# Attention and two feed-forward layers on one core: the first chunks' queries and keys loaded as 512 columns per half of the rows instead of 640 with zeros, and a new order of the program

## The chip, the cores and the metric

One Trainium2 chip; the program runs on one of its NeuronCores. A core has a matrix engine (TensorE, PE in the profile), a vector engine (VectorE, DVE), a scalar engine (ScalarE, ACT), a general engine (GpSimd, POOL) and a queue engine (SyncE, SP), which here issues every DMA. Each engine runs its own instructions in order and waits for the others by semaphores. The metric is the device time of one execution in microseconds, lower is better. The kernel before takes 863.84 us, the median of three runs (863.59 to 864.96).

## The reference

Block-causal attention (blocks of 64 positions) over 4 batches, 8 heads, 576 positions and 64 columns per head; then two feed-forward layers over the 2304 tokens, 512 wide, 2048 in between.

```python
scores = scale * np.matmul(q, k.transpose(0, 1, 3, 2))
scores = np.where(block_i >= block_j, scores, -1000000000.0)
attn = softmax(scores)                    # max subtracted, sum + 1e-9
x = np.matmul(attn, v)                    # heads put side by side: 2304 x 512
h = x @ w_in
x = (h * np.tanh(softplus(h))) @ w_out    # first layer
return np.square(np.maximum(x @ w_in2, 0)) @ w_out2   # second layer
```

All inputs and the output are float32.

## The kernel before

*Work.* The tokens go in six chunks of 384 through two layers, in twelve passes (`PASSES`). The first two chunks hold, of each batch, the first 192 positions (`LO`), and the other four the last 384 of one batch (`HI`). Attention of a `LO` chunk is done by `attention_lo` in float32, one pair of heads at a time: 2 chunks x 2 batches x 4 pairs are 16 calls. `HI` chunks go through `attention_hi`, with 16-bit high and low parts. A layer's products are also formed of 16-bit high and low parts, three matmuls each (L1352, L1464; L1385 and L1503 in the passes with seven products in place of eight), except for the first pieces of the first pass, in float32 (L1416, L1430). Weights arrive as packed integers, are decoded on DVE and ACT (L1149, L1150), weighed, split and written back to DRAM.

*One pair of heads in `attention_lo`.* L1042 loads queries and keys, 128 rows (64 per head) of 640 columns, L1043 the values. The columns are three blocks of queries (128 each) and the keys (64 and 192). A block of queries holds one head's columns in its 64 rows and zeros, which come with the load, in the other 64, so that a matmul over all 128 rows gives one head's scores (L1054; the third block has 64 queries of either head). L1055 adds the mask. DVE takes the maxima (L1059, L1060) and makes them the bias (L1061), ACT does three exponentials (L1064), DVE the reciprocal sums (L1067, L1069), ACT or DVE the scaling (L823, L825). Four transposes (L1077 to L1080) go through PE, L791 or L793 copies them out, and L1092 and L1093 multiply by the values.

*Buffers.* The loads of L1042 have six buffers (`R["qkl"]`), two in the tensor `qk` and four in `vs`, so the seventh load waits for the first scores. `qk` and `vs` are later reused by `attention_hi`.

*Order.* No loop sets the order. Every instruction is a task with an engine and dependences; a table (`PLAN`) gives the order of all tasks and the engine of those that could run on several (`planned`, L386). The table is unpacked at build time, and each engine gets its instructions in that order. `FIRST`, `SLACK`, `URGE` and the costs in `sch.add` belong to the planner that ran without the table; they don't act on the built program.

Of the kernel before, what the change touches and what calls it, by code (L numbers as in the profile page):

```python
# [68 lines left out]
def seg_len(tiles):  # L69
# [34 lines left out]
    ";%|0Ul6|_5RWHeL^qr0^BRJ(Jxlgw1vwDHvFT>G%pZ3K^dvpV9Ht20Klr@`msN5{uSoJwNZPpv4uUxHz<r%q77V1@UtNg21qxTcoxKdZ?3cX&wl~=IwRe2q`"
    "FS4q>T*2!La<^QD|1Oo;dJ?|6T?WaAaw#$BB30yZX(dm{bX}ki<JpCp1D3|<IQfxJKj;8?LE6bZSldEo>O}ojTg!O;T|0w>CuFStq7CFrovc4<Q|T>l$!Ge#"
    "*2TK}rG`w@Q940C)P7i4Q$EnUh|feUxm||o=Q;*oca}HsSY!EEn<MKLb(Xy<BlI2_qP68c^dGKY>Ye!W9q{u98g)aHf%xSOWdDLTqqT$d!nfB+Wuy86$Uj@|"
    "CE~fJ2k5$-b%*u8#NZNg;W6T{Pan}2vHJ$e0Ac&Jqud9sddfh32qfLD2jl>|d&pxT_L!{KR&oh`Ze|LIOdlDb*MpyX^g3-|dP{p*C%g4VEx@MLa=G@=m2$Oo"
    "*DbnC_SxQgNV{oQyt+Yq>U_!Jc}z3S0O`O<?Q|CV`^gq<t8=w2R^2Wa>NFW99mt+p`28lb;dAtCCS#?o_LBd}Tyo}GITN3@)PL~ujnYF}Xm1%uwiIDu6a7S9"
    "<*&o~2`C#v9{<2&nvNoVAIf}PA#ck-d0!@J8&FqSXMr7&cccZ#pRVKd4R$w?Ux~nIusxLhZ^~<?sZ5lQ^m!T2l^4xI`<6b7?Du(n9{pzMP%!zKJPPI>1Dh}F"
    "2gG%Zenv)?<Fu#sBORv0<Vj9?TOTL#uY=r_JdEwX+M)WO%(JyY%WI%_fc#gU(`q24KX+f$XXGifRi8v|F<Ee>Tx|02=5W0XX=~8^0qR;$PJUd5lIsu2BhrQQ"  # L110
    "9+G}kz9sl$lRipTEx^0|xw8%ruhjv1HNO2<`-A6pWYm3n7r30Jcj!RybhqBh?v~)brQAt{nT>aQfzKKG08wg$$7hnm`@!Yq+DU%Wp2YtSa<RX*lMBhUV{)^O"
    ")SKmYG~1vT>cya^vtFTZ>$Ti(qrKSGNM1#^Q)PjkPHh~?s&mEVTq7#z#YD1`oG0gl>QkhhZpNQA&AG(?9O};5c(5&3+mf|y<#at0UC-7$GP;#C*GAO0#?pt1"
    "IEXtpp>+f5PdRy#E5&&6bYfe`)u!?vEhW`JXCpkgl*~H?+4pKc?)BHxB%4pCQqw=gXCuKt6}f^MogyF4BnPamiMH0ZK-)TS&R{;*qMjbLzfyT$lR{gSx?WGq"
    "NL^T=A_&+H4{X!&GTJ-=+8-iUGl|Lrl4r}~y(84-dt|M>mwP#~#@;PuL2F;UcQ**?2lw;^XXVM!JBY1Nb)J&~+Xss-MD|TcI);p6$n8ay7+@YDL$=_pRb+a9"
    "BJvKXDzHna(PQm);xU~po~HBk4%w;Q&}|11*+EslN!~Tvz)gF0PjH^L)j`YuV1oI&#7?2=EwY<*67^s`o}54g*XrMPjdrDGt|oV8+V*f$C;3a;Qv>TFr#YyZ"
    "58u?{Qx|zaenI1Eaxr<>Le8gV=Tn{9%XgeLi)c?k=QG){9u{mxmYgH4<qPy(NyY9Cc50B5lhJsxj-_T*qDB^=?YC6lue2e49H|{_H#wWUtcSNhqu!own^QZ_"
    "Al`X;AB;6Z*OII6>%aOEIu6r|=o%Uj`)qdAk!Oi<8FUj6w-sx9V&zb3r4s+=K*n1AT`CfRhIlpyPp<&CkAZ=c$+Wuc{EseVZF_Xv&igj7XvnX>i2GP@b4<UH"
    "Hppm56)r=@ucDeC&`rmC>w82wm-^61-jzD!rotn0i0BsBvk3m~j`W)Nye7UWP1YZz+H|I(??r<Pq_RAX?SrtP5KrWj?`5cxkD%!W?Aed4v$SbYoebHfGw4<f"
    "`53^a4S2oXYyKhLIS6OXhw<0Iyz_WpK;F**5!>*6iX9f)en+SIuuQ37D@>n>2YSG%ztBCbq#mtO$ELsO74%dWakY>~9yMSSJXc5s8Vhpr@a=jkZ)x=0Ps9uL"
# [1779 lines left out]
```

## Time and profile before

| | |
|---|---|
| median of 3 runs | 863.84 us (863.59 to 864.96) |
| profiled execution: time, span | 863.41 us, 861.6 us |
| PE, DVE, ACT, POOL busy | 845.8, 759.8, 614.9, 63.2 us |
| PE weight loads busy | 606.5 us |
| DMA moved, mean rate | 217.24 MB, 252 GB/s |
| span in 40 slices, PE busy tenths | 7, then 38 of 9, then 7 |

The profile is one execution. Busy time is the time in which an engine has an instruction in it. Matmuls are pipelined, so a busy PE is not a PE at its peak; yet where it is busy all the time, another engine's delay has not reached it. DMA-issuing instructions don't count as busy for SP. Where an engine waited, the profile names the engine or the transfer that came last. The line numbers are those of the kernel before.

### The profile page before, as it was taken

To read this page: it belongs to the slowest core of one execution; us is meant where nothing else is said; L and a number is where in the kernel's file an instruction comes from. 1 tells how busy PE (TensorE), PEld (TensorE's weight loads), DVE (VectorE), ACT (ScalarE), POOL (GpSimd) and SP (SyncE) were. 2 spreads that over 40 slices of the span, in tenths; PEclk is the share of its full clock that TensorE was granted. 3 is DMA by queue.
4 is the path that set the end of the run, shared out by engine and by line. 5 is a ranking of instruction groups with operands and counts; after the bars stand their busy time and mean duration, and the time that the engine had idled before them with its cause. 6 is when DMAs were issued, how large, how long until landed. Compare 5 with 4: busy or idle time off the path is not lost.

```text
span 861.6 us, 19020 instructions
## 1 busy us (share of the span) xinstructions
PE 845.8 (98%) x7233; PEld 606.5 (70%) x7233; DVE 759.8 (88%) x1836; ACT 614.9 (71%) x1224; POOL 63.2 (7%) x70
## 2 busy tenths in 40 slices
...
GB/s 340 382 330 221 208 247 223 279 312 284 260 286 221 258 231 226 246 247 285 272 302 273 306 260 263 269 253 227 209 220 291 225 190 212 258 244 252 186 214 73
DMA packets 163931, 217.24 MB, mean 252 GB/s; under 512 B 107520, under 2 KB 125952, under 8 KB 163840
## 3 DMA queue, kind: packets, MB, share of 16 engines
...
q8 instruction: 56, 0.92, 0.4%
...
## 4 chain that ended last, share of the span: by engine, by line
PE 73%; ACT 6%; DVE 5%; DMA 4%; issue 1%; SPq 0%; ACTq 0%; DVEq 0%
PE acc L1464 28%; PE hp L1385 23%; PE hp L1352 10%; PE acc L1503 5%; PE bank L1018 3%; PE bank L909 2%; PE bank L1503 2%; DMA wspill<-arena 1%; DMA arena<-wspill 1%; ACT pad L933 1%; DVE st L922 1%; DVE arena L818 1%; DMA pt<-pb 1%; ACT h L1357 1%; DVE pb L818 1%
## 5 line engine op out<-in xcount | busy, mean ns | idle before, releaser
L1464 PE MATMUL acc<-g,arena 128*128 128x384 f16 x1560 | 301.5, 326 | 0.7 <-DMA arena<-wspill 0.7
L1464 PEld LDWEIGHTS <-arena 128*128 128x128 f16 x1560 | 147.1, 98 | 83.8 <-issue 3.4
L1385 PEld LDWEIGHTS <-arena 128*128 128x128 f16 x1194 | 101.1, 98 | 15.2 <-issue 1.5
L1352 PE MATMUL hp<-xt,first 128*128 128x384 f16 x528 | 102.7, 326 | 1.9 <-ACT h L1357 1.8
L818 DVE SCALAR_TENSOR_TENSOR g<-h,cst,g 128x768 f16<-128x768 f32 x72 | 73.7, 1024 | 6.9 <-ACT g L1121 4.0
L1352 PEld LDWEIGHTS <-first 128*128 128x128 f16 x528 | 49.5, 98 | 42.0 <-issue 10.9
L1385 PEld LDWEIGHTS <-first 128*128 128x128 f16 x816 | 69.5, 98 | 7.4 <-issue 0.5
L818 DVE SCALAR_TENSOR_TENSOR pb<-pad,st,pb 128x384 f16<-128x384 f32 (+2 forms) x96 | 71.6, 754 | 2.8 <-ACT pb L953 2.5
L933 ACT ACTIVATE pad<-bank,st,sq 128x448 f32<-128x448 f32 (+1 forms) x96 | 65.0, 680 | 12.6 <-DVE sv L839 4.9
L1352 PE MATMUL hp<-xt,arena 128*128 128x384 f16 x384 | 73.8, 326 | 0.0
L1385 PE MATMUL hp<-arena 128*128 128x192 f16 x660 | 67.3, 246 | 0.0
L953 ACT ACTIVATE pb<-pad,st 128x384 f16<-128x384 f32 (+2 forms) x81 | 57.1, 716 | 5.5 <-DVE st L945 2.5
L1406 ACT ACTIVATE h<-h,cst 128x576 f32<-128x576 f32 x40 | 30.9, 772 | 35.9 <-DVE h L1404 35.8
L922 DVE TENSOR_REDUCE st<-bank 128x1 f32<-128x448 f32 (+1 forms) x96 | 51.9, 570 | 3.0 <-PE bank L909 2.2
L1385 PE MATMUL hp<-xt,arena 128*128 128x192 f16 x534 | 54.1, 246 | 0.0
L1352 PEld LDWEIGHTS <-arena 128*128 128x128 f16 x384 | 36.2, 98 | 24.0 <-issue 0.8
L1385 PE MATMUL hp<-arena,first 128*128 128x192 f16 x480 | 50.4, 246 | 0.0
L1357 ACT ACTIVATE h<-hp,cst 128x384 f32<-128x384 f32 x76 | 41.8, 577 | 10.9 <-PE hp L1352 9.3
L1402 ACT ACTIVATE h<-hp,cst 128x192 f32<-128x192 f32 x40 | 16.6, 414 | 40.0 <-PE hp L1385 27.1
L1121 ACT ACTIVATE g<-h,cst 128x768 f16<-128x768 f32 x37 | 34.4, 930 | 13.5 <-PE acc L1464 9.2
L1210 DVE TENSOR_TENSOR arena<-arena 128x256 f32<-128x256 f32 x96 | 40.1, 418 | 0.8
L1503 PEld LDWEIGHTS <-arena 128*128 128x128 f16 x504 | 37.5, 98 | 0.0
...
## 6 DMA issues: line engine op xcount, KB each, us to landing
...
arena<-in_w_dram SPq DMA_DIRECT2D x27, 1023.8 KB, 6.9
...
```

Of the source, the lines that this page charges most:

```text
L818: return sch.add("DVE", c_dve(n) + 62 * ap, lambda: nc.vector.scalar_tensor_tensor(dst(), a(), s() if ap else s, c(), op0, op1), r=r, w=w, ...
L922: t = sch.add("DVE", c_dve(o1 - o0), lambda hd=hd: nc.vector.reduce_max(st.t[:, 2 * j + hd:2 * j + hd + 1], pp.t[hd][:, o0:o1], axis=AX.X) ...
L933: t = sch.add("ACT", c_act(o1 - o0, True, 3), lambda hd=hd: nc.scalar.activation(pf[hd].t[r0:, k0:k0 + o1 - o0], view(hd)[r0:, o0:o1], AF. ...
L953: "ACT": ("ACT", c_act(n, False, 1), lambda pb=pb, pv=pv, s=s: nc.scalar.activation(pb.t[:, 0:i + 1, 0, :], pv(), AF.Copy, scale=s()), False),
L1121: "ACT": ("ACT", c_act(n, False, 1), lambda: nc.scalar.activation(dst(0), src(), AF.Copy, scale=s()), False),
L1210: plus(ENG["ts"], 256, lambda e, o=o, x=x, y=y, op=op: e.tensor_tensor(b(o), b(x), b(y), op), [], [q])
L1352: nc.tensor.matmul(out=hp.t[:, 0:n], lhsT=w.t[:, f % 2, a, 128 * k:128 * k + 128], rhs=x.t[:, c, k, 0:n], start=k == 0 and i == 0, stop=k ...
L1357: sch.add("ACT", c_act(n, True, 1), lambda f=f, o=o, hp=hp: nc.scalar.activation(h.t[:, o * n:o * n + n], hp.t[:, 0:n], (AF.Mish, AF.Relu) ...
L1385: nc.tensor.matmul(out=bank.t[:, o:o + z], lhsT=lhs, rhs=x.t[:, c, ks[k], :], start=start and k == 0 and i == 0, stop=k == 1 and i == 2, s ...
L1406: sch.add("ACT", c_act(3 * z, False, 1), lambda: nc.scalar.activation(h.t[:, z:2 * n], h.t[:, z:2 * n], fn, scale=hs()), r=[(cst, (HS, j)) ...
L1464: nc.tensor.matmul(out=acc.t[:, 0:n], lhsT=wo.t[:, f % 2, a, 128 * m:128 * m + 128], rhs=g.t[:, c, f % 2 * n:f % 2 * n + n], start=f == 0 ...
L1503: nc.tensor.matmul(out=acc[bank].t[:, o:o + c1 - c0], lhsT=lhs, rhs=g.t[:, c, z * b + c0:z * b + c1], start=j == 0 and (bank, o) in first ...
```

## The change

*Loads.* Each pair of heads is loaded by two DMAs, one per head, into 64 rows of 512 columns each: rows 0 to 63 into columns 0 to 511, rows 64 to 127 into columns 128 to 639. The columns are in a new order, so that the outer 128 columns (0 to 127 and 512 to 639) hold one head's queries each. The other half's rows of those columns are zeroed once, at the program's start, by four memsets on DVE, for all six buffers. The matmuls read other columns and are the same in number and size; the scores now wait for two transfers.

```diff
+    for t in (qkt.rearrange("p (i c) -> p i c", c=960), vst.rearrange("p (i c) -> p i c", c=640)):
+        nc.vector.memset(t[0:64, :, 512:640], 0.0)
+        nc.vector.memset(t[64:128, :, 0:128], 0.0)
     nc.vector.memset(ones, 2.0 ** -13)
...
-        for t in (dma(lambda: nc.sync.dma_start(qs.t[:, 0:640], qk[b, h // 2]), 512 * 640, w=[qs]),
-                  dma(lambda: nc.sync.dma_start(vs.t, vd[b, h // 2]), 512 * 256, w=[vs])):
+        loads = [dma(lambda hd=hd: nc.sync.dma_start(qs.t[64 * hd:64 * hd + 64, 128 * hd:128 * hd + 512], qk[b, h // 2, 64 * hd:64 * hd + 64]),
+                     256 * 512, w=[(qs, hd)]) for hd in range(2)]
+        for t in loads + [dma(lambda: nc.sync.dma_start(vs.t, vd[b, h // 2]), 512 * 256, w=[vs])]:
...
-            for q, o, k, m in ((0, 0, 448, n), (256, n, 448, n), (128, 2 * n, 384, 64)):
+            for q, o, k, m in ((0, 0, 192, n), (512, n, 192, n), (384, 2 * n, 128, 64)):
...
-        steps = [sch.add("PE", 2 * c_f32(192) + c_f32(64) + 80.0, mm_s, r=[qs], w=[pp])]
+        steps = [sch.add("PE", 2 * c_f32(192) + c_f32(64) + 80.0, mm_s, r=[(qs, 0), (qs, 1)], w=[pp])]
...
-    FIRST = {"PE": 300.0, "ACT": 1300.0, "DVE": 700.0}
+    FIRST = {"PE": 300.0, "ACT": 1300.0, "DVE": 2400.0}
```

On the host, the array of queries and keys is laid out in 512 columns in place of 640, to match. The table of the order is replaced as a whole (its first two lines):

```diff
 PLAN = (
-    "c-m!}2YgjU^Y>@ZJp>Yx(5rybM4Etzs3=Vk6%{KYHmo3u<*_#eA4SDpKn1}DD*7lO2v!tCMCrXq37yahJqbJSclVrg!~gSoy(Q=D&QAHw{ATV&#7G5cAZ;aE"
+    "c-l>x37}2Y8ppr2&%XD%u6b6Z!H}X14N{6qq5)B)=ar&CX;d^IO&aBu)Jt<zuR#ONl88bfnKE4A8ZOt6dAQd1erv7051sBA_Fn5--}wK3-#IcOQdJts*>X_J"
...
```

*Where the order moves.* In the rows below an instruction has its line in its own version of the kernel; lines of the changed one are three to five higher in the same code. `qk` and `vs` are buffers of queries and keys, `in_w_dram` the packed weights (read into `arena` and `pad`), `in_vd_dram` the values, `acc`, `hp` and `bank` PSUM banks, `st` small statistics, `pt` the exponentials; xN means N in a row.

SP at the start of the program, before:

```order
L1042 DMA qk<-in_qk_dram 128x640 x2
L1042 DMA vs<-in_qk_dram 128x640 x2
L1139 DMA arena<-in_w_dram 128x4095
L1043 DMA pb<-in_vd_dram 128x256
L1042 DMA vs<-in_qk_dram 128x640 x2
L1043 DMA pb<-in_vd_dram 128x256
L1139 DMA arena<-in_w_dram 128x4095
L1042 DMA qk<-in_qk_dram 128x640 x2
```

and now:

```order
L1045 DMA qk<-in_qk_dram 64x512 x4
L1045 DMA vs<-in_qk_dram 64x512 x2
L1143 DMA arena<-in_w_dram 128x4095
L1045 DMA vs<-in_qk_dram 64x512 x6
L1047 DMA pb<-in_vd_dram 128x256 x2
L1143 DMA arena<-in_w_dram 128x4095
L1045 DMA qk<-in_qk_dram 64x512 x2
L1047 DMA pb<-in_vd_dram 128x256
L1045 DMA qk<-in_qk_dram 64x512 x2
```

Before, four whole loads stood ahead of the first weights and two behind; now six halves (three pairs of heads) stand ahead and six halves behind, the values come after them, and the second weights come after twelve halves and two loads of values in place of six loads and two of values. Over the whole program SP has 16 DMAs more.

DVE from its first instruction that reads data, before:

```order
L1059 TENSOR_REDUCE st_169<-acc_0_158 128x2
L1060 TENSOR_REDUCE st_169<-acc_0_158 128x1
L1061 TENSOR_SCALAR st_169<-st_169 128x3
L1059 TENSOR_REDUCE st_182<-acc_0_164 128x2
L1067 TENSOR_SCALAR st_169<-st_169 128x3
L1069 RECIPROCAL st_169<-st_169 128x3
L1060 TENSOR_REDUCE st_182<-acc_0_164 128x1
L1061 TENSOR_SCALAR st_182<-st_182 128x3
L768 COPY ident<-ident 128x64
L1149 CAST pad<-arena 128x1024
L1059 TENSOR_REDUCE st_202<-acc_0_177 128x2
```

and now (the four memsets of `qk` and `vs` stand ahead of everything on DVE):

```order
L1063 TENSOR_REDUCE st_180<-acc_0_165 128x2
L1064 TENSOR_REDUCE st_180<-acc_0_165 128x1
L1065 TENSOR_SCALAR st_180<-st_180 128x3
L1063 TENSOR_REDUCE st_192<-acc_0_174 128x2
L1064 TENSOR_REDUCE st_192<-acc_0_174 128x1
L1065 TENSOR_SCALAR st_192<-st_192 128x3
L1071 TENSOR_SCALAR st_180<-st_180 128x3
L1073 RECIPROCAL st_180<-st_180 128x3
L771 COPY ident<-ident 128x64
L1153 CAST pad<-arena 128x1024
L1063 TENSOR_REDUCE st_211<-acc_0_187 128x2
```

The second reduction of the second pair (`st_182` before, `st_192` now) moved ahead of the two small operations that wait for the first pair's exponentials; the cast of the first weights stays behind both, ahead of the third pair's reductions.

PE around the fifth pair's scores (`hp_124`), before:

```order
L1054 MATMUL hp_124<-vs 128x64
L1055 LDWEIGHTS above
L1055 MATMUL hp_124<-small,above 128x128
L1077 MATMUL acc_0_158<-ident,pt 128x128
L1078 MATMUL acc_0_158<-ident,pt 128x128
L1079 MATMUL acc_0_158<-ident,pt 128x128
L1080 MATMUL acc_0_158<-ident,pt 128x2x64
L1077 MATMUL acc_0_164<-ident,pt 128x128
L1078 MATMUL acc_0_164<-ident,pt 128x128
L1079 MATMUL acc_0_164<-ident,pt 128x128
L1080 MATMUL acc_0_164<-ident,pt 128x2x64
L1054 MATMUL acc_0_235<-vs 128x192 x2
```

and now:

```order
L1058 MATMUL hp_124<-vs 128x64
L1059 LDWEIGHTS above
L1059 MATMUL hp_124<-small,above 128x128
L1058 MATMUL acc_0_222<-vs 128x192 x2
L1058 MATMUL acc_0_222<-vs 128x64
L1059 LDWEIGHTS above
L1059 MATMUL acc_0_222<-small,above 128x128
L1081 MATMUL acc_0_165<-ident,pt 128x128
L1082 MATMUL acc_0_165<-ident,pt 128x128
L1083 MATMUL acc_0_165<-ident,pt 128x128
L1084 MATMUL acc_0_165<-ident,pt 128x2x64
```

Before, the first transposes followed the fifth scores, and the sixth came after two pairs' transposes; now the sixth scores (`acc_0_222`) stand ahead of them. PE's instructions are the same in number and kind over the whole program. ACT has 18 instructions more, 53 table loads among them in place of 51; DVE has 10 fewer and POOL 2 fewer, since copies, scalings and splits that can run on several engines are assigned anew. The extra pair of table loads stands among the activations that the kernel before runs at 187 to 216 us of its span.

## Rows read from the trace of the kernel before

**Rows 1.** The page, part 1: engine, busy us (share of the span), instructions.

```profile
...
PE 845.8 (98%) x7233; PEld 606.5 (70%) x7233; DVE 759.8 (88%) x1836; ACT 614.9 (71%) x1224; POOL 63.2 (7%) x70
```

**Rows 2.** By stretch: busy us by engine, PE's clock, DMA share, GB/s.

```profile
3.70:16.00 12.30, 10.39 (x63) 9.19 (x63) 8.06 (x30) 7.49 (x32) 0.00 (x0) 1.00 1.00 374
16.00:40.00 24.00, 23.16 (x152) 16.57 (x150) 23.06 (x87) 23.42 (x85) 0.00 (x0) 1.00 1.01 385
40.00:60.00 20.00, 19.58 (x101) 12.70 (x98) 18.74 (x43) 19.07 (x42) 0.00 (x0) 1.00 0.91 331
60.00:190.00 130.00, 127.65 (x828) 74.47 (x827) 122.30 (x308) 125.62 (x248) 11.54 (x14) 1.00 0.88 251
190.00:215.00 25.00, 24.57 (x170) 14.14 (x169) 24.05 (x60) 21.76 (x39) 4.32 (x5) 1.00 0.88 290
215.00:400.00 185.00, 184.05 (x1330) 107.53 (x1328) 170.35 (x409) 152.10 (x302) 19.08 (x17) 1.00 0.93 250
840.00:861.60 21.60, 16.42 (x217) 16.19 (x214) 14.42 (x27) 4.65 (x7) 1.39 (x1) 0.98 0.22 74
```

**Rows 3.** Waits up to 60 us: who waited <- for whom: us, times, longest.

```profile
...
PE acc L1054 <- DMA qk<-in_qk_dram: 3.7, 1, 3.7
...
PE hp L1054 <- DMA vs<-in_qk_dram: 1.8, 1, 1.8
...
DVE pad L1149 <- DMA arena<-in_w_dram: 1.1, 1, 1.1
...
PE bank L1054 <- DMA qk<-in_qk_dram: 0.4, 1, 0.4
```

**Rows 4.** Timeline to 13 us: start us, us, engine, line, out<-in, count, [idle before].

```profile
...
0.74 0.88 SPq L1042 DMA_DIRECT2D qk<-in_qk_dram  x2
...
1.10 0.11 DVE L772 MEMSET above<- 128x64 bf16 x1
1.17 0.09 DVE L773 MEMSET above<- 128x32 uint32 x1
...
5.81 0.56 DVE L1059 TENSOR_REDUCE st<-acc 128x2 f32<-128x384 f32 x1 [4.53 <-PE acc L1055]
...
6.80 0.42 ACT L1064 ACTIVATE pt<-acc,st 128x192 f32<-128x192 f32 x1 [4.79 <-DVE st L1061]
...
8.04 0.17 DVE L1067 TENSOR_SCALAR st<-st 128x3 f32<-128x3 f32 x1
...
8.34 0.19 DVE L1060 TENSOR_REDUCE st<-acc 128x1 f32<-128x64 f32 x1
...
9.96 0.75 DVE L1149 CAST pad<-arena 128x1024 f16<-128x1024 bf16 x1 [1.12 <-DMA arena<-in_w_dram]
...
11.15 1.08 PE L1054 MATMUL hp<-vs 128*128 128x192 f32 x6 [1.79 <-DMA vs<-in_qk_dram]
...
11.85 0.35 ACT L823 ACTIVATE pt<-pt,st 128x64 f32<-128x64 f32 x1 [0.89 <-DVE st L1069]
...
12.12 0.28 PE L1077 MATMUL acc<-ident,pt 128*128 128x128 f32 x1
```

**Rows 5.** DMA issues: out<-in, count, KB of one, median us from issue to landing.

```profile
...
arena<-in_w_dram SPq DMA_DIRECT2D x27, 1023.8 KB, 6.9
...
vs<-in_qk_dram SPq DMA_DIRECT2D x10, 320.0 KB, 6.9
...
pb<-in_vd_dram SPq DMA_DIRECT2D x16, 128.0 KB, 6.9
```

**Rows 6.** Line L1042, the loads: issue ns min/median/max; us from issue to landing.

```profile
...
L1042 SPq DMA_DIRECT2D vs<-in_qk_dram x10: 328/430/948, 1.7 to 51.1; - x10
...
DMA to landing us min/median/max: 2.9/6.9/8.9
```

**Rows 7.** Groups of ACT's instructions: busy us, mean ns of one, idle before.

```profile
...
L829 ACT ACT_TABLE_LOAD x15 | 19.2, 1283 | 0.3
```

**Rows 8.** Chain that ended last, in order of time: start us, us, what.

```profile
...
146.08 7.37 DMA pt<-pb
```

More of the change, by code (lines that the diff above doesn't have):

```diff
@@ L104 @@
[L104 to L119, printed above, removed]
@@ new lines @@
+    "13E=t!*jdzRhi56ck}^Hdxkw9%2PT=9^&4QdXP8_M$Z!7y(!<|(~Ww!Y|uOK?__yZhRALBY@0rSU$*EdxkXmsyBp*o);%rH$hEQ#eHZF$+FLg3W32jJ`=Q$k"
+    "9VS;wANh;(9+Xk~v)(VCOGmjBJLc;^86n+?%5VClbd`O)J}$rDvrA<L`VW@}<YGLsP=|2-bXK2_#b3x^GNGwFFW+-US@{;9-ihyj)z;DqEob22{_Oo!Tgn71"
+    ">nE?t586on$I0JmQyHP-@$Eojb&T9C^<|8Hub-j!r^J1|zN)kIGWl3%uzM|6$7>&{EF<+JeVfRh#F;P1)$$~F?jYkI*X~5Jp*%u-Mx)J(oHmn89i<)7_hETc"
+    "ua%!PpTCIw?}fi#)}GQv4BEe}x3h0Ax%;Aa#><zp>oW4RuWTb@_n_lmtW&vAdXw3=6Wif>o1QD3^&E2x@#!WHpu+*Gq=>xStJmp0>?oGI$kRU3OSelSvqgL8"
@@ new lines @@
+    "YHIFgy;`=DP3yI<cGe!UmU_BQFV$<cg)ESja*<wx9`{NU`Hf0gr593>zsdp~KvuS<KHJE-#P<xnQD%{6Q{@$+)QnixrS8^IY2V1X+F!;=Pco>7Opp>e4bNOJ"
+    "Z^#KmuZwh%N!kPpd*PKP<X0yU;YU4D>*MWb@aZo7)VxgAjleIr%2@JriTsxc<;a7)j+D`IuQZnzc%4S3jMx9j$?}PQCu8I}*=BcY19@5|>Z5q>a~Z48$!9uN"
+    "pCSkDkq^nRq4I=0t8I}rULT>dM(Q9U_kq4H17)BoBjd>YH}z$S<w0_EH2L$Qj+R04k>2N`%BrW4G#*Xo+b76{JLPCBeMIlGyEx}2a`R^DATndLy)ANCX1h`="
+    "U5HOt;(0$;mg|+s8;QKFAlOhmeYf=0V(n?}qQ?FtTiWpXHl(zd)8#JdD=qPKTd=Hw=_Uh-*>qim_fM7q<i`T?pbs(rPH)ju<z~GA|9+`+v?md{i%h>#y5s$B"
@@ new lines @@
+    "S|1$hueHqiaxB-{a`jZHBUexj7ZHn_K-jT*sr1mRwXW$XACM6psp?)te-wK3)OK>2t_LYP62()%sg9iAUSHD7wXU=W&(4+e(2?vQ3(l3Z^$$5mPNG^`<F!V3"
+    "_)L(txweusvAD9dkkh24_CtrJS|Io6qnvkwo-7ZOga6Wp^*ETKfi$E-PX%8~kkka$xL5B5J9qi~7pi`{)&pyAqY^8CWew#9EeH11C$DP4FBP<v=91@iMRYQ_"
+    "*#eXvN#4wrh-+oYk$ia;%^#PVa?sY~d57Hss^+2TaCt{#Flarju@1B!DCLOy8n|jOd{c?MS!oM&DKQ@)6{)EkL7B2-YfUmg2gJUaEW3#uI$%c-KO=kXgQkyc"
+    "bkaf1-XL}<+0~0I7dWj4Hnj$CZl{*6z^Xfl;VrCQ$YT?6>?H4)k8D3Gp&#7SL5g*=o)5Ba(3#}T1w^w5O@Gqm_A1!%FIx;k&BK!$$m`SPD|o3HeDb(mgrq{9"
@@ new lines @@
+    "P2R3x*9BzM@2qIZ{-10+qINu2PLa3pYBSJtDsjJD{sc8IB4cXE@8C@_dC(qSU(fr-)anfVPFI7LA931LFh7>}dDm3_!?~x*MX=mLaI6Mb-X}Zu>JwmUB@mSi"
+    "v5n*n{ZP+<IorsY)ZHue2N`Ow1?aq1-_UcYo5px*fc_V2SLjn{T7j&15j<E-Tt?||vT78#WkfZXdR>p5&+3yrH>Gl}0K0~Pf+xb*`>4PnoSbjB>O<bIdEmp3"
+    "Xm|&nisVzG{~P&n9?@N9Yk+8HqkBtEd6$!StLr41!g#qbuj^R;OFrh2gBhZfBd16{e7y9~^VI3(TBN^#4l~JNmt7rn8fPts7pv2sv_r;)?5l)dhZ4*3K8kaR"
+    ";y~GhzE$Wc@;QACc~u*$R)ODz<iIU5h00s5*Wr)vkX#XqmV!24YON@j4BJZv)+D!M`j>@BjKPH&u<=H$yNYN%hIO4_o+4s&1(oy-wcZ)+JAsZHVEZX_1{<i7"
@@ L193 @@
+    "Bf*DsWJyMwPy|W;5r-TJ$!Ox#*ktHPkSI=Flmt4h8Zn0*Z6rD(`!eB10!ryEpONV$NgGMWC{g@>6&ccP"
 )
```

168 lines of the change are left out of this document (84 added, 84 removed).

## The prediction

> **What bounds the kernel now.** I read the engines' busy time first. TensorE (PE) is busy 845.8 of 861.6 us [rows 1], so all its idle time together is 15.8 us, and no edit that leaves its instructions alone can win more. The profiled execution took 863.41 us: span plus 1.8 us around it. The three timed runs have a median of 863.84 (863.59 to 864.96), 0.43 above the profiled one.
>
> PE waits 3.7 us for its first data [rows 3]. The table by stretch says where it is idle after that [rows 2]: 1.91 us up to 16 us, 0.84 and 0.42 in the next two stretches, 2.34 between 60 and 190, 0.43 and 0.95 up to 400, and 5.18 in the tail, which drains the last outputs and isn't touched. The reader is to see a second thing there: from 16 to 60 us ScalarE (ACT) and VectorE (DVE) are as full as PE (23.42 and 23.06 of 24 us, then 19.07 and 18.74 of 20), and the DMA engines move 385 GB/s at a share of 1.01. So early on a late transfer, a late ACT and a late DVE all cost alike, and what is lost before 16 us isn't regained in the next forty.
>
> The waits of the first 60 us say what was late [rows 3]: PE waited 3.7 us for the first transfer of queries and keys, 1.8 for the fifth and 0.4 for a later one; DVE 1.1 for the first weights. The timeline shows how these hang together [rows 4]. The fifth load stands behind 1 MB of weights and lands at 11.15 us. PE takes its work in order, so the transposes of heads already done start only at 12.12. DVE stands in L1149 until the same weights land at 9.96; behind that stand the reductions of the third head, and behind those the reciprocal of the second, for which ACT waits 0.89 us until 11.85. ACT's first exponential is at 6.80; from there to 16 us it has 9.20 us and fills 7.49 [rows 2], so 1.71 are idle.
>
> **The change part by part.** *Loads.* A pair of heads took one transfer of 320 KB, 128 rows of 640 columns [rows 5]; now two of 128 KB, 64 rows of 512 each. For 16 pairs that is 5.24 against 4.19 MB, 1.05 MB less. At 385 GB/s this is 2.7 us of a full DMA system, spread over the first 51 us.
>
> First matmul: a first load lands 2.9 us after issue at the earliest [rows 6]. 327,680 bytes at 383 GB/s (I take the middle between the 374 and 385 of rows 2) are 0.86 us, so 2.04 are fixed. The second half is issued 0.44 us after the first (two issues in 0.88 us [rows 4]), at 1.18, and ends at 1.18 + 2.04 + 0.34 = 3.56 instead of 3.64: -0.1 us.
>
> Weights: before, four full loads go ahead of the first weights, now six halves (the order of SP above): 1.31 MB against 0.79, 0.52 MB less, 1.4 us. They land near 8.6 instead of 9.96. DVE reaches L1149 at 8.84 (9.96 less its idle 1.12), so its wait is gone, and with it most of ACT's 0.89 us before 11.85. I take 0.9.
>
> Heads five and six: through the fifth load 2.82 MB went before and 2.36 now (ten halves and the weights), 1.2 us less, so the 1.8 us wait falls to about 0.6. In PE's new order the sixth scores also precede the transposes. Through the sixth load it is 2.62 MB, 0.5 us before the 11.1 of the old fifth: 10.6, its scores take 1.1, and the transposes start near 11.7, 0.4 us earlier, with the sixth head already done, which before came behind them. PE is then no later than ACT, and ACT sets the pace.
>
> DVE's order: before, two small operations of head one (the first at 8.04) stand ahead of the second reduction of head two (8.34) and wait for ACT; now behind it. Head two's bias comes 0.3 us earlier.
>
> The start therefore gains on ACT 0.1 + 0.3 + 0.9 = 1.3 us, under its ceiling of 1.71. The later wait of 0.4 us for queries and keys goes too, since 14 loads before it are then 0.92 MB lighter (2.4 us): -0.4. Bounds: nothing, or 1.7 + 0.4 + the 0.1.
>
> No row shows a transfer into half of the partitions. The nearest rows, full ones, give 374 to 385 GB/s, and I take that rate, since the rows of vd with 128 KB land as fast as those of 320 KB (6.9 us both in the middle, in a full queue) [rows 5]. The other end is half of it, 192 GB/s, if 64 rows reach only half of what takes the bytes. That end is priced as a rival.
>
> *Zeroing.* Four memsets of 2x256 and 2x512 elements stand first on DVE. One of 64 columns starts 0.07 us ahead of the next [rows 4], about 1.1 ns a column, so 1536 cost 1.7 us. DVE was idle for 4.53 us before its first reduction at 5.81, which hides them. Uncovered they would cost 1.7.
>
> *SP.* 16 more issues of 0.43 us [rows 6] are 6.9 us over 51 us. Loads take 6.9 us from issue to landing against 2.9 for the first, so they stand in the queue for bytes, not for SP: nothing. Uncovered, the last loads come up to 6.9 us late, and PE would wait for part of it.
>
> *Order everywhere else.* PE executes the same matmuls. ACT has 18 more instructions and DVE 10 fewer; two of ACT's are table loads of 1.28 us [rows 7]. The extra pair stands where ACT had 3.24 idle us of 25 (190 to 215 us) [rows 2]: nothing; uncovered 2.6. The other way, an order without PE waits from 16 to 400 us would give back 0.84 + 0.42 + 2.34 + 0.43 + 0.95 = 5.0 us. An order alone doesn't tell a wait, so I take 0, the value nearest to the old rows, and keep -5.0 and +2.6.
>
> Sum: -1.3 - 0.4 = -1.7 us. Against the profiled execution 861.7, against the median 862.1. I forecast the middle, 861.9.
>
> **The rule that speaks against it.** The rows of a full queue say 385 GB/s for transfers to all 128 partitions [rows 2]. The Trainium skill, page "SBUF — State Buffer", sections "Door 1: The DMA port swizzle (why [64,N] ≈ [32,N])" and "Can I just issue two DMAs to hit both halves?", says that partitions 0 to 63 reach only half of the DMA ports, that such a transfer moved 196 GB/s where a full one moved 328, and that two for the two halves went only 6% faster than one. No run here shows it yet. By that rule the sum would be the first rival below instead of a gain; the traces as they stand don't bear it out or deny it.
>
> **The rivals.** *Halves at half the rate (slower).* At 192 GB/s a half takes 0.68 us. The first head is complete at 0.74 + 2.04 + 2 x 0.68 = 4.14 (+0.5). Six halves end at 6.9, the weights (2.74 us) at 9.6, the sixth head's two halves, ten to twelve, at 13.7, its scores at 14.8, against 12.12 for the transposes before. The sixth head's 1.1 us is done by then, so PE stands 1.6 us behind. All 32 halves take 21.8 us against 13.8, 8 us more of a queue that is full to 40 us; I charge 0.5 of it to later waits for weights: 863.84 + 2.1 = 865.9. It decides from the rate at which the sixth load lands where the fifth did, 11.1 us: 1.57 MB in 11.1 - 2.78 - 2.74 = 5.6 us, 282 GB/s. Below that the start loses. For it: 64 rows are half of the partitions. Against: loads to both halves of the partitions are in flight together, with full ones between them.
>
> *The gain is given back (same).* ACT and DVE start sooner, but PE's idle 2.34 us between 60 and 190 us may be set by waits that don't begin with the loads: the chain of waits holds a transposing transfer of 7.37 us there [rows 8]. A lead would end at one of those: 863.84 less a few tenths, 863.5.
>
> *The new order also closes gaps.* If half of the 5.0 us goes beside the start's gain: 859.4.
>
> **How the numbers follow.** Forecast 0.42 (its own range 860.6 to 863.1: the start between half and all of its ceiling, and half a microsecond of new waits), half rate 0.24, given back 0.22, gaps closed 0.12. A measurement of this kernel can tell about 0.2%, 1.7 us, from no change: faster lies below 862.1, slower above 865.6. Of the forecast's case six parts in ten lie below 862.1, so faster is 0.25 + 0.12 + a little of the given-back = 0.40. The half-rate case reaches from 864 to 868, so 0.15 of it is slower; with 0.05 for table loads or memsets without cover, slower is 0.20; same is 0.40. The range cuts off the lower half of the closed gaps and the upper third of the half-rate case: 859.4 to 866.2.
>
> **What would show it.** Right: PE's first matmul at 3.5 to 3.8 us; DVE doesn't wait at the first cast of weights, which starts below 9.2; PE's wait at the fifth head under 1 us and the first transposes before 11.9; ACT idle under 1 us from its first exponential to 16 us; no wait for queries and keys after 40 us. Wrong: the first matmul at 4.1 or later and the sixth scores after 13.5 (half rate); DVE's first reduction after 6.2 (memsets without cover); a new PE wait behind ACT near 200 us of a table load's length; all signs of the start right and PE's idle time from 60 to 400 us larger than the 3.7 us of before (2.34 + 0.43 + 0.95) (given back). If none of the start's signs is there and the time is still under 862, I was right for a wrong reason.

## The result and the profile after

The changed kernel takes 869.77 us (median of 6 runs, 867.08 to 873.57) against 863.72 for the kernel before on the same chip: 1.0069 times as long, interval 1.0047 to 1.0091. It is slower by some 6 us; the forecast was 861.9, the range ended at 866.2. The profiled execution took 869.89 us, its span 868.1.

The page's first part, engine, busy time and instructions, answers to [rows 1]:

```profile
PE 849.0 (98%) x7233; PEld 609.1 (70%) x7233; DVE 761.9 (88%) x1826; ACT 626.6 (72%) x1241; POOL 60.0 (7%) x68
```

The span grew by 6.5 us: PE is busy 3.2 us longer with the same matmuls and idle for 19.1 us in place of 15.8. The table by stretch says where (columns as in [rows 2]):

```profile
3.70:16.00 12.30, 8.65 (x32) 8.45 (x33) 4.51 (x19) 4.56 (x21) 0.00 (x0) 0.88 0.97 270
16.00:40.00 24.00, 21.45 (x157) 16.46 (x156) 21.24 (x75) 21.33 (x82) 0.00 (x0) 0.99 1.02 312
40.00:60.00 20.00, 19.40 (x83) 11.87 (x82) 17.49 (x49) 16.68 (x43) 0.00 (x0) 1.00 0.98 331
60.00:190.00 130.00, 128.06 (x805) 73.95 (x805) 126.45 (x311) 124.83 (x252) 13.30 (x13) 1.00 0.86 246
190.00:215.00 25.00, 24.97 (x193) 14.70 (x193) 24.22 (x57) 23.50 (x44) 4.57 (x5) 1.00 0.85 303
215.00:400.00 185.00, 184.76 (x1335) 108.58 (x1332) 175.53 (x418) 156.28 (x308) 15.39 (x15) 1.00 0.95 255
400.00:846.00 446.00, 444.77 (x4417) 358.40 (x4416) 375.66 (x866) 272.70 (x487) 23.45 (x23) 1.00 0.82 247
```

Of the kernel before, the last stretch, for which no row was shown:

```profile
400.00:846.00 446.00, 445.96 (x4462) 361.71 (x4461) 382.87 (x882) 261.15 (x476) 26.34 (x23) 1.00 0.80 245
```

Up to 60 us PE idles 3.70 + 3.65 + 2.55 + 0.60 = 10.5 us; before it was 6.87 [rows 2]: 3.6 more. From 60 to 400 it idles 2.2 against 3.7, from 400 to 846 1.2 against 0.04. So the loss is made in the first 60 us. The last columns say what is wrong there: the DMA engines are as full as before (share 0.97 and 1.02) and move 270 and 312 GB/s, where they moved 374 and 385.

The waits of the first 60 us answer to [rows 3]:

```profile
PE acc L1058 <- DMA qk<-in_qk_dram: 4.1, 1, 4.1
...
PE hp L1058 <- DMA vs<-in_qk_dram: 3.3, 1, 3.3
DVE pad L1153 <- DMA arena<-in_w_dram: 2.6, 1, 2.6
ACT pt L1068 <- DVE st L1073: 2.6, 1, 2.6
...
PE bank L1096 <- DMA pb<-in_vd_dram: 1.3, 1, 1.3
```

The last one, for values, ends at 36.91 us and is half of the 2.55 us that PE idles between 16 and 40.

And the timeline of the start, SP's issues among it, answers to [rows 4]; SPq rows give the time that the issues took, not the transfers:

```profile
0.73 2.49 SPq L1045 DMA_DIRECT2D qk<-in_qk_dram  x4
...
4.05 1.94 PE L1058 MATMUL acc<-qk 128*128 128x192 f32 x6 [4.05 <-DMA qk<-in_qk_dram]
4.54 0.58 SPq L1143 DMA_DIRECT2D arena<-in_w_dram  x1
5.17 4.14 SPq L1045 DMA_DIRECT2D vs<-in_qk_dram  x6
...
7.70 1.91 PE L1058 MATMUL acc<-vs 128*128 128x192 f32 x6
...
9.36 2.78 SPq L1047 DMA_DIRECT2D pb<-in_vd_dram  x2
...
11.82 0.74 DVE L1153 CAST pad<-arena 128x1024 f16<-128x1024 bf16 x1 [2.62 <-DMA arena<-in_w_dram]
12.37 0.33 SPq L1143 DMA_DIRECT2D arena<-in_w_dram  x1
...
12.99 1.97 PE L1058 MATMUL hp<-vs 128*128 128x192 f32 x6 [3.30 <-DMA vs<-in_qk_dram]
...
16.52 1.04 PE L1058 MATMUL acc<-vs 128*128 128x192 f32 x6
17.45 0.28 PE L1081 MATMUL acc<-ident,pt 128*128 128x128 f32 x1
```

SP issues almost without a break until 9.9 us, at first a half every 0.64 us; the first weights go out at 4.54 (2.61 before) and land at 11.79 (9.94), the second ones go out at 12.37 (5.39). PE computes three heads and then waits 3.3 us for the fourth; the first transposes come at 17.45 in place of 12.12.

The single packets in the trace say more of the weights. Of their 128 packets of 8,190 bytes 120 have ended by 9.32 us, much as before (9.25). The last eight end as late as 11.07 (9.56 before). So a few late packets hold the landing of the whole transfer; what holds them, no run shows.

The line of the loads answers to [rows 6]:

```profile
L1045 SPq DMA_DIRECT2D vs<-in_qk_dram x20: 465/591/1073, 3.3 to 58.5; - x20
```

An issue of a half takes 0.59 us in the middle, that of a whole load of 128 rows took 0.43. It isn't the 64 rows alone: the weights, 128 rows, took 0.58 here too, right behind a half (4.54), against 0.43 before. Meanwhile the queue ran short: the row of the changed kernel from 6.0 to 6.8 us, then that of before.

```profile
6.00:6.80 0.80, 0.80 (x4) 0.80 (x4) 0.67 (x2) 0.00 (x0) 0.00 (x0) 1.00 0.55 123
```
```profile
6.00:6.80 0.80, 0.80 (x4) 0.80 (x4) 0.67 (x3) 0.00 (x0) 0.00 (x0) 1.00 1.00 390
```

PE's longer busy time is its clock. Granted in the stretch behind the wait of 3.3 us:

```profile
12.94:16.35 3.41, 3.36 (x12) 3.36 (x13) 1.50 (x9) 1.54 (x8) 0.00 (x0) 0.50 1.07 332
```

0.50 is the lower of its two levels, 1.2 of 2.4 GHz; PE had been idle for the 3.3 us just before. Over the 3.36 busy us this is 1.7 us of work lost. Before, the row of that stretch says 1.00 [rows 2]. Another 0.9 is the third head at 7.70: its matmuls take 1.91 us, as those of the first two heads in either kernel, where before the third took 1.04:

```profile
7.33 1.04 PE L1054 MATMUL acc<-vs 128*128 128x192 f32 x6
```

The table by stretch says 1.00 there, but the trace has no record of the clock that early: its first one, at 1.00, stands at 9.53 us here and at 7.26 before, and without a record the table writes 1.00. The third head lies behind that record before and ahead of it now. A head's matmuls take 1.97 us where 0.50 is on record (the fourth head, 12.99), so the third head most likely ran at the lower level.

### The profile page after: what moved, and what is told of

Same layout as the page of the kernel before. It is cut to its first block, busy times and chain, and to the rows that moved or that the text cites. A ratio compares the mean times of both kernels' runs of the same rounds, so it can differ in the third digit from the quotient of the medians.

```text
span 868.1 us, 19034 instructions
## 1 busy us (share of the span) xinstructions
PE 849.0 (98%) x7233; PEld 609.1 (70%) x7233; DVE 761.9 (88%) x1826; ACT 626.6 (72%) x1241; POOL 60.0 (7%) x68
## 4 chain that ended last, share of the span: by engine, by line
PE 69%; DVE 11%; ACT 10%; DMA 4%; issue 4%; SPq 1%; POOL 0%; ACTq 0%; DVEq 0%; POOLq 0%
PE acc L1468 24%; PE hp L1389 20%; PE hp L1356 10%; PE acc L1507 4%; PE bank L912 2%; PE bank L1021 2%; PE bank L1507 2%; PE acc L1434 2%; ACT pad L936 1%; ACT wsq L1166 1%; ACT h L1361 1%; DMA pb<-in_vd_dram 1%; PE hp L1420 1%; ACT L1361 1%; DVE g L821 1%
## 5 line engine op out<-in xcount | busy, mean ns | idle before, releaser
L1468 PEld LDWEIGHTS <-arena 128*128 128x128 f16 x1560 | 146.3, 98 | 84.4 <-issue 5.3
L1389 PEld LDWEIGHTS <-arena 128*128 128x128 f16 x1194 | 101.0, 98 | 13.4 <-issue 0.8
L821 DVE SCALAR_TENSOR_TENSOR pb<-pad,st,pb 128x512 f16<-128x512 f32 (+2 forms) x96 | 71.6, 749 | 1.6 <-ACT pb L956 1.0
L1356 PEld LDWEIGHTS <-arena 128*128 128x128 f16 x384 | 36.5, 98 | 25.2 <-issue 1.5
L1125 ACT ACTIVATE g<-h,cst 128x768 f16<-128x768 f32 x40 | 37.1, 928 | 7.2 <-PE acc L1468 4.0
L912 PE MATMUL bank<-q 64*128 64x448 f16 (+2 forms) x384 | 37.4, 305 | 0.5 <-ACT pad L936 0.4
```

The source lines that it names most:

```text
L821: return sch.add("DVE", c_dve(n) + 62 * ap, lambda: nc.vector.scalar_tensor_tensor(dst(), a(), s() if ap else s, c(), op0, op1), r=r, w=w, ...
L912: nc.tensor.matmul(out=pp.t[hd][:, o:o + k1 - k0], lhsT=qh.t[rows, u, a:a + 128], rhs=qh.t[rows, w, nq + k0:nq + k1], start=p == 0, stop=p ...
L1125: "ACT": ("ACT", c_act(n, False, 1), lambda: nc.scalar.activation(dst(0), src(), AF.Copy, scale=s()), False),
L1356: nc.tensor.matmul(out=hp.t[:, 0:n], lhsT=w.t[:, f % 2, a, 128 * k:128 * k + 128], rhs=x.t[:, c, k, 0:n], start=k == 0 and i == 0, stop=k ...
L1389: nc.tensor.matmul(out=bank.t[:, o:o + z], lhsT=lhs, rhs=x.t[:, c, ks[k], :], start=start and k == 0 and i == 0, stop=k == 1 and i == 2, s ...
L1468: nc.tensor.matmul(out=acc.t[:, 0:n], lhsT=wo.t[:, f % 2, a, 128 * m:128 * m + 128], rhs=g.t[:, c, f % 2 * n:f % 2 * n + n], start=f == 0 ...
```

## The experiments

Two theories at first: A, half rate (a transfer into 64 neighbouring rows moves about half the bytes per time), and B, the new order (its late waits). "Old" is the order of before, "new" that of the change. Every ratio is to runs of the kernel before on the same chip.

| kernel | order | loads | median us | ratio, interval |
|---|---|---|---|---|
| change | new | neighbouring halves | 869.77 | 1.0069 (1.0047 to 1.0091) |
| full_new | new | whole, with zeros | 864.19 | 1.0010 (0.9997 to 1.0024) |
| half_old | old | neighbouring halves | 870.07 | 1.0081 (1.0059 to 1.0103) |
| every2_new | new | halves in every second partition | 868.18 | 1.0054 (1.0037 to 1.0070) |
| every2_old | old | halves in every second partition | 867.07 | 1.0048 (1.0029 to 1.0067) |
| issue2_old | old | two of 128 rows x 320 | 869.00 | 1.0055 (1.0040 to 1.0071) |
| two_queues_new | new | change, three issues by ACT | 871.01 | 1.0077 (1.0062 to 1.0091) |
| every2_two_queues | new | every second, three issues by ACT | 867.81 | 1.0049 (1.0031 to 1.0066) |
| mixed_old | old | 6 whole, then 10 every second | 864.27 | 1.0006 (0.9993 to 1.0019) |
| mixed_half_old | old | 6 whole, then 10 neighbouring | 869.53 | 1.0063 (1.0044 to 1.0081) |
| first6_half_old | old | 6 neighbouring, then 10 whole | 866.85 | 1.0040 (1.0025 to 1.0056) |
| every2_pool_new | new | every second, values by POOL | 869.38 | 1.0062 (1.0048 to 1.0077) |
| dummy_old | old | whole, 16 useless transfers | 867.78 | 1.0045 (1.0031 to 1.0060) |
| dummy4_sp | old | whole, 4 useless ones by SP | 867.44 | 1.0043 (1.0021 to 1.0065) |
| dummy4_act | old | the same 4 by ACT | 864.23 | 1.0002 (0.9989 to 1.0016) |
| dummy4_pool | old | the same 4 by POOL | 864.59 | 1.0007 (0.9994 to 1.0020) |

**The order or the loads: full_new, half_old.** full_new, against the change:

```diff
-        loads = [dma(lambda hd=hd: nc.sync.dma_start(qs.t[64 * hd:64 * hd + 64, 128 * hd:128 * hd + 512], qk[b, h // 2, 64 * hd:64 * hd + 64]),
+        loads = [dma(lambda hd=hd: nc.sync.dma_start(qs.t[:, 0:640], qk[b, h // 2]) if hd == 0 else None,
```

> The new order with whole loads: where the first half was issued, one transfer of 128 rows of 640 columns with the zeros in it; nothing where the second half was; no zeroing by DVE. Theory A (64 neighbouring rows take about half the rate; in the changed kernel halves land 0.6 us apart in a full queue, 131,072 bytes / 0.6 = 218 GB/s): the start comes back, first matmul 3.7, first weights by 9.2 in place of 11.8, PE's wait after the third head under 1.5 in place of 3.3 us, time 862.5 to 864.5. Theory B (the new order costs the time by itself, above all by its waits after 400 us, 1.2 us): 867 or more, start no better than half. Between them, 864.5 to 867: both.

half_old, against before (with the change's layout, columns and zeroing):

```diff
-dma(lambda: nc.sync.dma_start(qs.t[:, 0:640], qk[b, h // 2]), 512 * 640, w=[qs])
+dma(lambda: [nc.sync.dma_start(qs.t[64 * hd:64 * hd + 64, 128 * hd:128 * hd + 512], qk[b, h // 2, 64 * hd:64 * hd + 64]) for hd in range(2)], 512 * 512, w=[qs])
```

> The order of before with the new loads: each load of 128 rows x 640 becomes two of 64 rows x 512 issued one behind the other, with the four zeroings first on DVE and the matmuls' new columns. Theory A: eight halves now stand ahead of the first weights, 8 x 0.6 us and 2.5 us of weights behind the first 2.5 us, so the weights land after 12 and the fifth head's scores after 12.5 (9.94 and 11.15 before); 866 to 870. Theory B: the start as before, 862.5 to 865.

The order can't be told from nothing (+0.10%), the loads in the old order cost 0.81%: the whole loss is the loads'. The table by stretch of full_new, the same seven columns:

```profile
3.70:16.00 12.30, 11.02 (x63) 9.71 (x63) 8.59 (x33) 8.06 (x37) 0.00 (x0) 1.00 1.03 390
16.00:40.00 24.00, 23.69 (x152) 16.89 (x152) 23.37 (x83) 23.87 (x84) 0.00 (x0) 1.00 1.02 396
...
400.00:846.00 446.00, 444.75 (x4449) 360.69 (x4450) 373.96 (x859) 272.54 (x485) 24.23 (x24) 1.00 0.81 246
```

Up to 60 us PE idles 3.70 + 1.28 + 0.31 + 0.00 = 5.3 us, 1.6 less than before: with whole loads the new order does gain at the start, the first weights landing at 8.76. It gives 1.2 of it back in its own waits from 400 to 846, which the changed kernel has too.

**Which rows: every2_new, every2_old.** Against the change; in the order of before likewise. The outer blocks are zeroed in all rows.

```diff
-nc.sync.dma_start(qs.t[64 * hd:64 * hd + 64, 128 * hd:128 * hd + 512], qk[b, h // 2, 64 * hd:64 * hd + 64])
+nc.sync.dma_start(qs.t[hd:128:2, 128 * hd:128 * hd + 512], qk[b, h // 2, 64 * hd:64 * hd + 64])
```

> The changed kernel with a head's 64 rows put into every second partition in place of 64 neighbours (same bytes, number and order of transfers; the sums over rows are the same sums in another order); the outer blocks are zeroed in all rows, so the first load waits for a zeroing, some 0.5 us. Theory A (it is which partitions): halves land 0.35 us apart in a full queue, the weights by 10, and the time is 862.5 to 865.5. Theory C (it is 64 rows, 2 KB pieces or SP's issue of 0.59 us each, whatever the partitions): 0.6 us apart as before and 868 to 872.

> The same every-second-partition loads in the order of before (two issued one behind the other). Theory A: near before, 863 to 866 (0.5 us for the zeroing that the first load waits for, and SP's second issue). Theory C: as the order of before with neighbouring halves, 866 to 870.

The rate is as theory A has it. In the trace of every2_new the halves behind the weights land at 10.41, 10.75, 11.09, 11.44, 11.76 and 12.10, 0.34 us apart (131,072 bytes in 0.34 us: 386 GB/s); in the changed kernel at 12.35, 12.95, 13.55, 14.15, 14.68 and 15.31, 0.59 apart (222 GB/s). The single pieces of 2,048 bytes take 84 ns against 156 on average (from 6.7 to 16 us). The medians fell by 1.6 and 3.0 us; the intervals overlap with those of the neighbouring halves, so the first fall isn't clear of noise and the second barely is. Neither time fell to where theory A put it: 868.18 where it said 865.5 at most, and 867.07 where it said 866. Of the 4 us above full_new the first load's wait for the zeroing (issued at 1.16) is 0.4. In the profiled executions, 2.5 us apart, the whole difference is PE's idle time at the start, 8.0 us up to 60 us against 5.3 in full_new; the rows of every2_new:

```profile
3.70:16.00 12.30, 9.92 (x55) 9.02 (x55) 7.57 (x29) 6.94 (x30) 0.00 (x0) 1.00 0.93 321
16.00:40.00 24.00, 22.07 (x147) 16.24 (x147) 21.51 (x83) 22.60 (x86) 0.00 (x0) 1.00 0.97 364
40.00:60.00 20.00, 20.00 (x97) 12.57 (x96) 18.89 (x41) 18.70 (x43) 0.00 (x0) 1.00 0.93 329
```

**What is left: issue2_old, two_queues_new, every2_two_queues, mixed_old.** The first diff is issue2_old against before; the second makes two_queues_new of the change and every2_two_queues of every2_new; the third is mixed_old against before.

```diff
+dma(lambda: [nc.sync.dma_start(qs.t[:, i:i + 320], qk[b, h // 2, :, i:i + 320]) for i in (0, 320)], 512 * 640, w=[qs])
```
```diff
-nc.sync.dma_start(
+(nc.scalar if hd and qs.idx < 3 else nc.sync).dma_start(
```
```diff
+dma(lambda: [nc.sync.dma_start(qs.t[hd:128:2, 128 * hd:128 * hd + 512], qk[b, h // 2, hd:128:2, 128 * hd:128 * hd + 512]) for hd in range(2)]
+    if qs.idx >= 6 else nc.sync.dma_start(qs.t[:, 0:640], qk[b, h // 2]), 512 * 512, w=[qs])
```

> The kernel of before with each load of 128 rows x 640 columns issued as two of 128 rows x 320: twice the issues, the same bytes, all partitions. Theory C (what is left when every second partition is used, some 3.5 us, is SP's pace at the start: 64-row halves are issued 0.64 us apart, 131,072 bytes / 0.64 = 205 GB/s, while the queue is still empty): issues of 128 rows took 0.43, so eight of them for 1.31 MB still outrun the bytes; the weights are issued 1.9 us later but land at 9.9 to 10.8 (9.94 before); 863.5 to 865.5. Theory D (a transfer has a cost of its own, so that twice as many cost whatever their pace): 866 to 868.

> The changed kernel with the second halves of the first three pairs issued by ACT, idle then, in place of SP. Theory C with half rate: SP issues the first weights at 2.6 in place of 4.54; the two halves of a pair go side by side to different partitions, so the first matmul comes at 3.4 to 3.7 and the weights land at 9 to 10.5 in place of 11.8; the later halves stay slow; 866 to 868.5. Half rate alone, SP's pace without weight: 869 to 871, weights no earlier than 11.

> Both cures together: a head's rows in every second partition, and the second halves of the first three pairs issued by ACT. If half rate and SP's pace are the whole cost: 863 to 865.5 (868.2 with every second partition alone), weights landing by 9.2. If something else in the halves costs (their number, the zeroing that the first load waits for): 866 or more.

> The order of before; the first load of each of the six buffers whole, 128 rows x 640 with the zeros, so no zeroing and the start as before; the ten later ones as two halves of 512 columns in every second partition. What the smaller loads bring by themselves: 0.65 MB less between 7 and 55 us, at 385 GB/s 1.7 us of DMA time, of which PE waited 0.4. Theory A and C: 862.7 to 864.3, the queue being full by then. If it is 865 or more, halves cost in a full queue too, by SP's issues.

Three of these four went against theory C. Loads of all 128 partitions, only split in two, cost 0.55%: 869.00 us, even above the 868 that theory D allowed. Issuing three halves from ACT sent the first weights out at 2.63, but they landed at 11.37 and the time didn't fall. Here too 120 of the 128 packets of weights have ended by 9.13 us and the last at 10.58; what holds the last ones is open. Together with every second partition the time was 867.81, no better than 868.18 without: in the profiles PE idles 1.0 us less (17.1 and 18.1) and is busy 2.2 us longer with the same matmuls (849.0 and 846.8). The first record of the full clock stands at 16.44 us there, at 9.14 without ACT's issues. mixed_old came out as expected: with a start as before, ten pairs of halves and 0.65 MB less cost and bring nothing that can be told. So theory D doesn't hold as it was worded: twice as many transfers cost at the start, not in a full queue.

**Count, or size, or place: dummy_old, mixed_half_old, first6_half_old, every2_pool_new.**

```diff
+dma(lambda: [nc.sync.dma_start(qs.t[:, 0:640], qk[b, h // 2]),
+             nc.sync.dma_start(spare[:, qs.idx % 8:qs.idx % 8 + 1], qk[b, h // 2, :, 0:1])], 512 * 640, w=[qs])
```

> The kernel of before, its loads whole, and behind each of the 16 a useless transfer of 128 rows x 4 bytes into a spare column: SP's count of transfers goes up as in the change, the bytes don't. Theory E (SP may have eight transfers in flight, each issue waits for the landing of the eighth before it; twice as many transfers fill the eight places, so the next ones, weights above all, are issued later: the second weights at 5.39 before, 9.29 with loads split by columns, 12.37 in the changed kernel): second weights issued at 8 or later, first ones landing after 11, 866 to 869.5. Theory F (what costs is that pieces of 1,280 to 2,048 bytes move slower, not the count): 863.5 to 865.

mixed_half_old and first6_half_old load whole if `qs.idx < 6`, in neighbouring halves otherwise, or the other way about:

> The order of before; the first load of each of the six buffers whole, the ten later ones as neighbouring halves of 512 columns. What half rate costs behind a clean start: ten pairs at 1.2 in place of 0.85 us are 3.5 us of a full queue between 15 and 55 us. If the later halves carry a share of the loss: 865 to 867.5. If the whole loss is of the first six loads: 863.5 to 865, as with every second partition (864.3).

> The opposite: the first load of each of the six buffers as neighbouring halves with the zeroing, the ten later ones whole. If the loss is of the start: 868 to 871, near the 870.1 of all halves. If it is spread: 865 to 867.5.

```diff
-nc.sync.dma_start(vs.t, vd[b, h // 2])
+nc.gpsimd.dma_start(vs.t, vd[b, h // 2])
```

> Every second partition in the new order, and the values' 16 loads issued by POOL, whose transfers have places of their own. Theory E: SP's eight places hold only halves and weights, so the second weights are issued before 9 (10.49 with every second partition alone) and the time falls from 868.2 to 864.5 to 867. If the places don't matter: 867.5 to 869.5.

dummy_old: the count alone costs 0.45%, with the first weights landing at 12.12 and the second ones issued at 9.70, as theory E had it. mixed_half_old is the cleanest pair of the study: it and mixed_old differ only in which partitions ten pairs of halves go to (and in the order of the rows in DRAM, which follows from it), and the ratios are 1.0063 and 1.0006, more than I had expected of half rate. Its start is as good as before; the loss sits in a wait at 32 us, which mixed_old doesn't have, and again in the clock behind it (0.50 from 35.40 us). Waits of mixed_half_old up to 60 us, then two stretches of it, behind them one of mixed_old:

```profile
PE bank L1055 <- DMA vs<-in_qk_dram: 2.8, 2, 2.5
ACT pad L1149 <- DMA arena<-in_w_dram: 2.6, 1, 2.6
```
```profile
16.00:40.00 24.00, 20.97 (x133) 15.06 (x132) 19.31 (x70) 21.23 (x79) 0.00 (x0) 0.93 1.05 324
...
35.40:38.80 3.40, 3.40 (x9) 1.95 (x8) 3.15 (x12) 3.37 (x15) 0.00 (x0) 0.50 1.07 308
```
```profile
16.00:40.00 24.00, 23.14 (x151) 16.69 (x153) 23.04 (x88) 23.45 (x87) 0.00 (x0) 1.00 1.00 364
```

first6_half_old, at 866.85, lost less than I expected of the start; it lies where I had put a loss that is spread. every2_pool_new failed as a test: the second weights were issued at 10.29 (10.49 without), and POOL's values went ahead of the first weights, which landed at 13.51 in place of 10.10.

**SP's line, or the eight places: dummy4_sp, dummy4_act, dummy4_pool.** SP issues a transfer only when the one eight before it has landed: in the kernel before, the fifth lands at 9.94 us and the thirteenth goes out at 10.00, the sixth lands at 10.27 and the fourteenth goes out at 10.38. These are the eight places. Against before, with `sync`, `scalar` and `gpsimd`:

```diff
+dma(lambda: [nc.sync.dma_start(qs.t[:, 0:640], qk[b, h // 2]),
+             qs.idx < 4 and nc.sync.dma_start(spare[:, qs.idx:qs.idx + 1], qk[b, h // 2, :, 0:1])], 512 * 640, w=[qs])
```

> The kernel of before with a useless transfer of 128 rows x 4 bytes behind each of the first four loads alone, issued by SP. It carries both suspects: SP's time (four more issues of 0.46 us ahead of the first weights, issued at 4.5 in place of 2.61) and the eight places (four of them taken). With the useless transfers behind all 16 loads the time was 867.8; if the first four carry most of it: 866 to 868; if the later ones do: 863.5 to 865.5.

> The same four, issued by ACT, which is idle then; its transfers take places out of the same eight. SP's time per issue as the cause: first weights issued at 2.6 again and the time back at 863.5 to 865. The eight places as the cause: the first weights, now the ninth transfer, wait for the first landing (3.7), the next for the second, second weights at 7 or later; as the four from SP within 1 us.

> The same four, issued by POOL, whose transfers have places of their own: neither suspect is left. SP's time or places as the cause: 863 to 864.8, second weights issued at 5.4. If 866 or more, the small transfers themselves hold up the queues.

Timeline of dummy4_sp, then of dummy4_act:

```profile
4.51 0.43 SPq L1141 DMA_DIRECT2D arena<-in_w_dram  x1
...
11.63 0.74 DVE L1151 CAST pad<-arena 128x1024 f16<-128x1024 bf16 x1 [2.68 <-DMA arena<-in_w_dram]
...
12.77 1.65 PE L1056 MATMUL hp<-vs 128*128 128x192 f32 x4 [2.65 <-DMA vs<-in_qk_dram]
```
```profile
0.76 1.85 ACTq L1044 DMA_DIRECT2D spare<-in_qk_dram  x4
...
4.03 0.33 SPq L1141 DMA_DIRECT2D arena<-in_w_dram  x1
...
9.61 0.74 DVE L1151 CAST pad<-arena 128x1024 f16<-128x1024 bf16 x1 [0.37 <-DMA arena<-in_w_dram]
...
10.80 1.08 PE L1056 MATMUL hp<-vs 128*128 128x192 f32 x6 [0.98 <-DMA vs<-in_qk_dram]
```

Four transfers of 512 bytes in SP's line, ahead of the first weights, cost 0.43%; the same four through ACT or POOL cost nothing that can be told. With ACT the eight places were taken, and the first weights did wait for one (until 4.03), which cost nothing: taken places alone don't carry the loss, and my theory E falls for this start. In the changed kernel the second weights go out at 12.37 us, right behind the landing of the transfer eight before (12.35); no run shows what that wait costs. What is shown is that more transfers in SP's own line at the start cost the time.

Most of the cost comes through the clock. With SP, PE waits 2.65 us for the fifth pair (0.98 with ACT), and behind that wait it is granted 0.50. The first part of the page of dummy4_sp, and its table by stretch:

```profile
PE 848.6 (98%) x7233; PEld 609.5 (70%) x7233; DVE 760.8 (88%) x1836; ACT 615.0 (71%) x1224; POOL 63.3 (7%) x70
```
```profile
12.77:18.50 5.73, 5.73 (x24) 5.52 (x26) 4.60 (x19) 4.60 (x18) 0.00 (x0) 0.50 1.02 398
3.70:16.00 12.30, 9.58 (x42) 9.40 (x43) 6.34 (x22) 5.63 (x25) 0.00 (x0) 0.84 0.97 357
16.00:40.00 24.00, 23.46 (x157) 17.60 (x156) 21.48 (x81) 21.90 (x86) 0.00 (x0) 0.94 0.97 355
40.00:60.00 20.00, 20.00 (x94) 12.43 (x92) 19.37 (x51) 19.32 (x44) 0.00 (x0) 1.00 0.93 332
```

PE idles 7.0 us up to 60 us, as before (6.9), but is busy 848.6 us with the same matmuls, 2.8 us longer than before and 2.5 longer than with ACT (846.1). That is most of the 3.9 us by which its span, 865.5 us, is longer than before. Its ten runs spread from 864.63 to 874.84.

Two things stay open. The weights were issued 0.5 us later with SP than with ACT and landed 2.0 later (11.61 and 9.59). Half of their packets have ended by 8.26 us with SP and by 7.63 with ACT, the last at 11.25 and 9.15; so again it is the last ones that come late, and I don't know what held them. And SP's time per issue was not separated from the small transfers' standing in that line between the loads.

## Why the prediction was wrong

- **Rate of a half (the step that failed first).** I took the full rate because 128 KB rows of values landed as fast as 320 KB ones; but those go to all 128 partitions, and the 6.9 us that both showed were time in a full queue. Measured: 222 GB/s for halves in 64 neighbouring rows, 386 in every second partition. The Trainium skill, page "SBUF — State Buffer", section "Door 1: The DMA port swizzle (why [64,N] ≈ [32,N])", says that partitions 0 to 63 reach half of the ports and that a transfer of 1 MiB to them moved 196 GB/s. The two measurements here agree that the partitions decide the rate, though the halves here are 128 KB and go to the two halves of the partitions in turn. I had half rate as a rival at 0.24.
- **"SP: 0".** The second step that failed. A load that stands in a queue for bytes hides its issue (mixed_old); in the first 7 us the queue is not always full (share 0.55 from 6.0 to 6.8 us, 1.00 there before), and fifteen issues stand ahead of the second weights where nine did. I also took 0.44 us per issue from whole loads; here issues take 0.59. My bound "uncovered, PE would wait for part of it" was the right end, and I left it out of the range. Alone it is worth 0.43 to 0.55% (dummy4_sp, dummy_old, issue2_old, and every2_old, where some 0.4 us are the wait for zeroing); half rate alone behind a clean start 0.57% (mixed_half_old less mixed_old). Together they are 0.69 to 0.81%, less than their sum. What each costs inside the changed kernel isn't separated: with the rate cured 0.54% is left, and no run takes all of SP's extra issues out of it.
- **The rival's price.** 865.9 was 4 us short. Its half rate was right for the six halves ahead of the weights: 6.9 forecast, 6.62 measured. But it gave the weights 2.74 us behind them, and they took 5.2 (11.79 in place of 9.6), so that the sixth head's halves came at 15.31 in place of 13.7. And it left out the clock: 1.7 us behind the wait of 3.3, and 0.9 at the third head.
- **First matmul** 3.56 by the forecast, 4.05 measured (4.14 in the rival): the second half is issued at 1.37, not 1.18, and landed 2.54 us later, not 2.38. (The middle of 374 and 385 is 379.5, not 383; the 0.86 us of a whole load stay.) **Weights** 8.6, measured 11.79. **Heads five and six** ready by 11.7, measured 17.45. The first matmul lay between my signs for right (3.8) and for half rate (4.1); the sixth scores (16.52) came out as I had written for half rate, and the cast of weights, the wait of PE and the first transposes failed their signs. Only the wait for queries and keys after 40 us was gone, as forecast.
- **Order elsewhere 0.** Right: full_new, +0.10%. There the start's gain is 1.6 us of PE's idle time, and the late waits take 1.2 of it back, by waits of the new order after 400 us, not in the transposing transfers where my "given back" rival put it.
- **Later wait for queries and keys, -0.4, and 1.05 MB less.** The one PE wait of 0.4 us did go, in the changed kernel too. In mixed_old, where the start is as before, it went and the time didn't move (1.0006): fewer bytes brought nothing that can be told.
- **Zeroing 0.** The four memsets took 1.5 us, and DVE still stood idle for 2.85 us before its first reduction at 6.13, inside the 6.2 that I had allowed, since it waits for PE. No run tried it alone.
